# A list scheduler's table and gates changed in a fused attention, expert and MLP kernel, with one layer in plain float32

## The chip, the cores and the metric

The kernel runs on one core of one Trainium2 chip. A core has a tensor engine (PE, its weight loads are shown as PEld), a vector engine (DVE), a scalar engine (ACT), GpSimd (POOL), a queue that issues transfers (SP), and 16 DMA engines that all queues share. The metric is the device time of one execution in microseconds (us). The time before is the median of three runs, 1221.68 us.

## What is computed

Three stages follow each other: attention, a router with capacity that gives each of 1792 tokens to one of 8 experts, and one MLP on all tokens.

```python
x = attn(q, k, v)                      # 1792 tokens x 768
logits = x @ w_gate                    # 1792 x 8
for idx in argsort(-logits.flatten()): # best pair first
    tok, e = idx // 8, idx % 8
    if assigned[tok] >= 0 or counts[e] >= 224: continue
    assigned[tok] = e; counts[e] += 1
for e in range(8):
    out[e's tokens] = relu(x[e's tokens] @ w1[e]) @ w2[e]   # 768 -> 1024 -> 768
h = out @ w_in                         # 768 -> 2048
return (h * cos(h)) @ w_out            # 2048 -> 768
```

## The kernel before, in words

The kernel records steps, each with an engine, an estimated duration, and what it reads and writes, and a list scheduler (`Plan.run`) then writes them out in an order for each engine. That order is final: on the chip every engine takes its instructions in this order and waits at each for what it needs. There are two plans. The first holds attention and the start of the router; the second, `moe`, everything from the first expert on.

**The second plan.** Eight router *phases* each find the tokens of one expert. Phases 0 and 1 search by counting (`quick`), phases 2 to 7 by bisection (`slow`). `route(t, behind)` records phase t, the load of the expert's number, two gathers of 112 rows of x each into `xr` (POOL) and their transposes into `xe`. `expert(t, j)` has a first layer of 8 blocks of 18 matmuls 128x128 by 224 columns (`acc<-xe,wx`) and a second one of 6 blocks of 24 (`acc<-gh,wx`, 224 columns). Two experts make a group, and `mlp` then takes the group's 448 columns: 16 blocks of 18 (`acc<-x2h,wx` and `x2l`, below M1), 6 blocks of 48 (`acc<-gh,wx` and `gl` with 448 columns, below M2).

**Three products.** Every such matmul is done as three in fp32r: each operand is split in a rounded part and a rest. An expert's weights come as float32 into `ws` (ring of 4), ACT writes the rounded part and DVE the rest into `wx` (ring of 4): `weights`, lines 1176 to 1194. The MLP's weights were split before and are loaded as they are.

**A bisection phase** writes its 56 KB table `vm` to DRAM (`rows`), and eight copies on SP read it back, each spread over 16 partitions (`AB<-rows`, lines 987 to 992). Then eight search steps follow: DVE compares (`oh<-AB`, two halves), ACT counts, DVE makes `ind`, PE sums over partitions (`rt<-ind,bd`), DVE sets the next bound. At the end come `M`, a prefix sum, `rel`, `pv` and 16 small matmuls (`rt<-pv,oh`) that give `idx`, the row numbers for the gathers.

The step costs of these transfers are numbers in the code: an SP issue 0.5 us, a copy 0.4 us of bus, and 1.1 us from the bus to landing for all transfers.

```python
            if s.dma is not None:
                bus = max(bus, st + (1.1 if w[0] == "SP" else 2.0)) + s.dma
                s.end = bus + 1.1
```

Phases 2, 4 and 6 may begin only after a step named by `behind`: the last matmul block of the group's second expert (`chain[-1]`). Two `memset`s on POOL write one element of the third and fourth buffer of `ws` after the first gathers.

Of the kernel before, what the change touches and what calls it, by code (L numbers as in the profile page):

```python
# [23 lines left out]


class Step:
    __slots__ = ("ways", "after", "before", "late", "wait", "ready", "end", "eng", "dma", "start", "rush", "mode", "pad")

    def __init__(self, ways, dma):
        self.ways, self.dma, self.rush = ways, dma, 0.0  # L30
        self.after, self.before = {}, []
        self.wait, self.ready, self.end, self.late = 0, 0.0, 0.0, None

# [17 lines left out]
class Plan:  # L51
# [51 lines left out]
        hi = lo + 1 + sum(s * (n - 1) for s, n in free)  # L103
        return x.name, p, p + n, lo * size, hi * size

    def add(self, ways, reads, writes, dma=None):

        if self.group is not None:
            self.group.append((ways[0], reads, writes))
            return  # L110
        s = Step(ways, dma)
        s.mode, s.pad = None, self.pad * (ways[0][0] == "PE")
        if ways[0][0] == "PE" and isinstance(reads[0], bass.AP):
            w = reads[0]
            s.mode = (w.partition_size() <= D, 32 if w.free_size() <= 32 else 64 if w.free_size() <= 64 else 128)
        s.rush = self.rush + self.ahead * (ways[0][0] != "DVE")
        for x in reads:
            self.touch(s, x, False)
        for x in writes:
            self.touch(s, x, True)  # L120
        self.steps.append(s)
# [47 lines left out]
    def run(self, order, prefer=0.0, edge=1.0, lag=2.6, hold=0.7, by=6.0, queue=9e9, more=0.0,  # L169
            same=0.0):  # L170

        for s in self.steps:
            s.wait = len(s.after)
            for t in s.after:
                t.before.append(s)
        nxt = dict(order)  # L180
        for s in reversed(self.steps):
            e, d = s.ways[0][0], min(w[1] for w in s.ways)
            d += lag if s.dma is not None else 0.0
            late = 0.0
            for t in s.before:
                late = min(late, t.late - SYNC.get((e, t.ways[0][0]), 0.17) - (
                    edge if e != t.ways[0][0] else 0.0))
            if s in nxt:
                late = min(late, nxt[s].late - more * d)
            s.late = late - d  # L190
        for s in self.steps:
            s.late -= s.rush
        free, bus, mode = {}, 0.0, None
        avail = [s for s in self.steps if s.wait == 0]
        idx = {s: i for i, s in enumerate(self.steps)}
        out = []
        while avail:
            best = None
            for e in ("PE", "DVE", "ACT", "POOL", "SP"):
                least = free.get(e, 0.0) if e != "SP" else max(free.get(e, 0.0), bus - 1.1 - queue)  # L200
                mine = [(max(least, s.ready), s, w) for s in avail for w in s.ways if w[0] == e]
                if not mine:
                    continue
                good = []
                for st, s, w in mine:
                    f = st + w[1]
                    if len(s.ways) > 1:
                        f += prefer * w[1] * (e == "DVE")
# [24 lines left out]
            if s.dma is not None:  # L233
                bus = max(bus, st + (1.1 if w[0] == "SP" else 2.0)) + s.dma
                s.end = bus + 1.1
            out.append((st, idx[s], w[2]))
            for t in s.before:
                t.ready = max(t.ready, s.end + SYNC.get((s.eng, t.ways[0][0]), 0.17) + t.pad)
                t.wait -= 1
                if t.wait == 0:  # L240
                    avail.append(t)
        assert len(out) == len(self.steps)
        for _, _, f in sorted(out, key=lambda o: o[:2]):
            f()
# [457 lines left out]
class Router:  # L702
# [276 lines left out]
    def slow(self):  # L979
# [5 lines left out]
        v.tensor_tensor(vm, vt, P["m"].unsqueeze(1).to_broadcast([CP, E, NCOL]), op=ALU.min)  # L985
        rows, sync = self.rows, nc.nc.sync
        nc.add([("SP", 0.5, lambda: sync.dma_start(rows.rearrange("e (p c) -> p e c", c=NCOL), vm))], [vm], ["rows"],
               dma=1.5)
        for e in range(E):
            nc.add([("SP", 0.5, lambda e=e: sync.dma_start(V[16 * e:16 * e + 16],  # L990
                                                           rows[e:e + 1].to_broadcast([16, NCOL * CP])))],
                   ["rows"], [V[16 * e:16 * e + 16]], dma=0.4)
        b, KX, ti, h = P["b"], P["KX"], P["ti"], NCOL * CP // 2
        for s in range(8):
            src = P["b0"]
# [101 lines left out]
C1 = 6.28125  # L1097
C2 = 2.0 * math.pi - C1
TUNE_B = (1.75, 0.8, 2.6, 0.6, 7.0, 9e9)
RUSH = (15.0, 0.0, 5.0)  # L1100
QUICK = (0, 1)
WARM_B = 24
GATE = 2
AHEAD = 100.0
TURN = 5
GROUPS = [[0, 1], [2, 3], [4, 5], [6, 7]]


def moe(tc, P, R, ident, x_rows, w1, w2, w_in, w_out, out, narrow):

    nc = tc.nc
    with ExitStack() as ctx:
# [12 lines left out]
        obuf = ring("o", 1, [128, PT])  # L1125
        rows = ring("xr", 2, [CP, DM])
        xe = cst.tile([128, KD, PT], F32R, name="xe")
        xo = cst.tile([CP, 4, DM], F32, name="xo")
        x2h = cst.tile([128, KD, PT], F32R, name="x2h")
        x2l = cst.tile([128, KD, PT], F32R, name="x2l")  # L1130
# [8 lines left out]
        def route(t, behind):  # L1139
# [9 lines left out]
            xr = []  # L1149
            for h in range(2):  # L1150
                x = rows()
                P.add([("POOL", 1.03, lambda x=x, h=h: nc.gpsimd.indirect_dma_start(  # L1152
                    out=x, out_offset=None, in_=x_rows,
                    in_offset=bass.IndirectOffsetOnAxis(ap=idx[t][:, h:h + 1], axis=0)))], [idx[t]], [x], dma=0.96)
                xr.append(x)
            R.close()
            if t == 0:
# [5 lines left out]
                P.rush = RUSH[0]  # L1163
                for _ in range(GATE):
                    stage()
                for _ in range(4 - GATE):
                    o = stage()[0:1, 0, 0:1]
                    P.add([("POOL", 0.04, lambda o=o: nc.gpsimd.memset(o, 0.0))], xr, [o])
            for q in range(3):
                p = turn() if t or q < 2 else acc()  # L1170
                for j in range(2):
# [3 lines left out]
                        P.tensor.transpose(p[:, o:o + CP], xr[h][:, d * 128:(d + 1) * 128], ident[0:CP, 0:CP])  # L1175
                src = p[:, 0:PT].rearrange("p (j s) -> p j s", j=2)
                hi, lo = xe[:, 2 * q:2 * q + 2, 0:CAP], xe[:, 2 * q:2 * q + 2, CAP:PT]
                sc.activation(hi, src, AF.Copy)
                v.tensor_tensor(lo, src, hi.bitcast(F32), op=ALU.subtract)

        def weights(src, c0, n, keys):

            s, x = stage()[:, 0:n], parts()[:, 0:n]
            hi, lo = x[:, :, 0], x[:, :, 1]

            def load():
                w = src()
                nc.sync.dma_start(s, w[:, c0:c0 + 128].rearrange("(k p) n -> p k n", p=128))

            P.add([("SP", 0.46, load)], keys, [s], dma=n * 0.182)  # L1190
            P.add([("ACT", 0.093 + n * 0.1067, lambda: nc.scalar.activation(hi, s, AF.Copy)),  # L1191
                   ("DVE", 0.07 + n * 0.0667, lambda: nc.vector.tensor_copy(hi, s))], [s], [hi])
            v.tensor_tensor(lo, s, hi.bitcast(F32), op=ALU.subtract)
            return hi, lo
# [19 lines left out]
        def expert(t, j):  # L1214
# [1 line left out]
                return lambda: w[bass.ds(ev[t], 1)].rearrange("o k n -> (o k) n")  # L1216

            for f in range(K1):
                hi, lo = weights(of(w1), f * 128, KD, [f"ev{t}"])
                p = acc()[:, 0:CAP]  # L1220
                for d in range(KD):
                    block(lambda: three(p, hi[:, d], lo[:, d], xe[:, d, 0:CAP], xe[:, d, CAP:PT], d == 0, d == KD - 1))
                a, b = hT[:, f, 0:CAP], hT[:, f, CAP:PT]
                sc.activation(a, p, AF.Relu)
                v.scalar_tensor_tensor(b, p, 0.0, a.bitcast(F32), op0=ALU.max, op1=ALU.subtract)
# [59 lines left out]
            nc.gpsimd.memset(apart, 0.0)  # L1285

        P.shared = False
        narrow.plan(P, cst, len(narrow.todo))
        behind = None

        def fetch(t, step=None):
# [6 lines left out]
        for grp in GROUPS:  # L1298
            for j, t in enumerate(grp):
                if j:  # L1300
                    fetch(t)
                expert(t, j)
            behind = chain[-1]
            mlp(grp, lambda: fetch(grp[-1] + 1, behind))
        P.run(zip(chain, chain[1:]), *TUNE_B)

# [64 lines left out]
```

## Time and profile before

| what | us |
|---|---|
| median of three runs (1220.99 to 1222.58) | 1221.68 |
| the profiled execution, its own time | 1224.71 |
| its span, first to last instruction | 1222.9 |
| PE busy in the span | 1142.1 |
| DVE busy | 852.9 |
| ACT busy | 657.5 |

The profiled execution took 1.8 us more than its span, and 3.0 us more than the median of the runs. Attention fills the first 365 us, the switch to the experts lies from 365 to 450 us, and the rest is a row of experts and MLP groups in which PE is nearly always busy. A busy PE isn't PE at its peak: a matmul's record is longer than the distance to the next one.

### The profile page before, as it was taken

The page shows a single profiled execution, that of the slowest core. Times are in us where ns is not written, and L with a number is a line of the kernel's source. Part 1 is how long each engine was busy: PE and PEld are TensorE (multiplying, and loading weights), DVE is VectorE, ACT ScalarE, POOL GpSimd, SP SyncE. Part 2 cuts the span into 40 slices and gives each one's busy share as a digit, 9 for nine tenths or more (in the row PEclk, how much of TensorE's full clock was granted, in tenths as well). Part 3 has the DMA queues.
Part 4 walks back from the last instruction along what each step waited for, and adds up shares of the span by engine and source line. Part 5 has one row for each costly group of instructions (what it writes and reads, how often), then busy time and mean ns, then how long its engine had stood idle before and what let it go on. Part 6 is the DMA issues. An engine that isn't in the chain of part 4 may idle for free.

```text
span 1222.9 us, 23588 instructions
## 1 busy us (share of the span) xinstructions
PE 1142.1 (93%) x8712; PEld 947.5 (77%) x8712; DVE 852.9 (70%) x2335; ACT 657.5 (54%) x1576; POOL 150.3 (12%) x287
## 2 busy tenths in 40 slices
PE   7999999999985989998999999899999899999996
PEld 4555655565543889887899988799988789999996
DVE  6998999999958865794576498277579458546401
ACT  5976877776643533781455384255468155435400
POOL 5532324241000000000001000002000001100001
PEclk8999999999995889999999999899999999899999
DMA  8357666766642656779468767838776856766761
GB/s 203 115 165 226 209 209 189 247 232 219 215 141 63 166 154 205 236 241 245 163 164 241 209 214 251 257 91 228 218 245 233 240 192 162 207 197 211 233 216 60
DMA packets 181395, 241.86 MB, mean 198 GB/s; under 512 B 14176, under 2 KB 156960, under 8 KB 175136
## 3 DMA queue, kind: packets, MB, share of 16 engines
q1 hardware_dynamic: 178720, 229.35, 61.1%
q0 software_dynamic: 2560, 11.01, 3.2%
q8 instruction: 68, 1.11, 0.4%
q14 instruction: 47, 0.39, 0.1%
HBM read 203.71 MB, written 36.52 MB: 196 GB/s over the span
## 4 chain that ended last, share of the span: by engine, by line
PE 50%; DVE 27%; DMA 13%; ACT 6%; issue 3%; POOL 1%; SPq 1%; POOLq 0%; DVEq 0%; ACTq 0%
PE acc L47 35%; DVE r L47 4%; DVE cm L47 4%; PE po L47 3%; PE st L47 3%; DMA xr<-x,idx 3%; DVE na L47 3%; ACT oh L47 3%; DVE oh L47 3%; DMA AB<-rows 3%; PE s L47 2%; PE dn L47 2%; PE tr L47 2%; DVE wx L47 1%; DMA ws<-in_moe_w_dram 1%
## 5 line engine op out<-in xcount | busy, mean ns | idle before, releaser
L47 PE MATMUL acc<-gh,wx 128*128 128x224 f32 (+1 forms) x1952 | 374.9, 317 | 0.0
L47 PEld LDWEIGHTS acc<-gh,wx 128*128 128x128 f32 x1952 | 286.5, 195 | 24.7 <-issue 13.1
L47 PE MATMUL acc<-x2h,wx 128*128 128x448 f32 x768 | 223.6, 369 | 0.0
L47 DVE TENSOR_TENSOR wx<-ws,wx 128x768 fp32r<-128x768 f32 (+1 forms) x112 | 120.0, 1071 | 64.5 <-ACT wx L1191 64.5
L1191 ACT ACTIVATE wx<-ws 128x768 fp32r<-128x768 f32 (+1 forms) x112 | 104.7, 936 | 109.6 <-PE acc L47 69.6
L47 PEld LDWEIGHTS acc<-x2h,wx 128*128 128x128 f32 x768 | 144.6, 188 | 15.5 <-issue 3.1
L47 ACT ACTIVATE oh<-oh 128x896 bf16<-128x896 bf16 x96 | 90.4, 942 | 107.0 <-DVE oh L47 105.5
L47 PE MATMUL acc<-gl,wx 128*128 128x448 f32 (+1 forms) x400 | 146.1, 365 | 0.0
L47 PE MATMUL acc<-x2l,wx 128*128 128x448 f32 x384 | 140.7, 366 | 0.0
L47 PE MATMUL acc<-xe,wx 128*128 128x224 f32 x1152 | 137.1, 280 | 0.6 <-DVE wx L47 0.5
L47 PEld LDWEIGHTS acc<-xe,wx 128*128 128x128 f32 x1152 | 134.4, 196 | 1.3 <-DVE wx L47 0.7
L47 ACT ACTIVATE pf<-st 112x448 f32<-112x448 f32 x192 | 93.4, 537 | 38.7 <-PE st L47 36.5
L47 DVE TENSOR_REDUCE cm<-s 128x1 f32<-128x448 f32 x168 | 99.5, 616 | 5.2 <-PE s L47 3.8
L1152 POOL DMA_INDIRECT xr<-x,idx x16 | 17.7, 1107 | 652.7 <-issue 215.9
L47 DVE TENSOR_SCALAR oh<-AB,b 128x896 bf16<-128x896 f32 x96 | 61.6, 683 | 50.5 <-DMA AB<-rows 34.4
L47 PE MATMUL st<-qq,kk 64*112 64x448 f32 x576 | 92.3, 391 | 2.3 <-ACT pf L47 2.2
L47 ACT ACTIVATE r<-r 128x448 f32<-128x448 f32 x128 | 72.8, 573 | 36.5 <-DVE r L47 35.1
L47 PE MATMUL po<-pf,vr 112*64 112x448 f32 x384 | 84.5, 560 | 0.0
L47 PEld LDWEIGHTS acc<-gl,wx 128*128 128x128 f32 x400 | 77.4, 193 | 5.2
L47 PEld LDWEIGHTS acc<-x2l,wx 128*128 128x128 f32 x384 | 72.2, 188 | 5.8
L47 PEld LDWEIGHTS st<-qq,kk 64*112 64x112 f32 x576 | 49.4, 171 | 25.7 <-ACT pf L47 10.1
L47 DVE SCALAR_TENSOR_TENSOR na<-nr,na 128x384 int32<-128x384 int32 (+1 forms) x112 | 68.0, 632 | 0.5
(237 smaller groups left out, 1662.5 us busy)
## 6 DMA issues: line engine op xcount, KB each, us to landing
wx<-w_in SPq DMA_DIRECT2D x64, 768.0 KB
wx<-w_out SPq DMA_DIRECT2D x48, 1024.0 KB
ws<-in_moe_w_dram SPq DMA_DIRECT2D x64, 384.0 KB
ws<-in_moe_w_dram SPq DMA_DIRECT2D x48, 512.0 KB
nr<-in_moe_w_in_dram SPq DMA_DIRECT2D x32, 384.0 KB
w_in<-nr SPq DMA_DIRECT2D x32, 384.0 KB
nr<-in_moe_w_out_dram SPq DMA_DIRECT2D x24, 512.0 KB
w_out<-nr SPq DMA_DIRECT2D x24, 512.0 KB
```

Source lines behind the costliest of these rows:

```text
L47: self.plan.add([(self.eng, self.plan.cost(self.eng, name, out, r, kw), lambda: f(*args, **kw))], r, w)
L1152: P.add([("POOL", 1.03, lambda x=x, h=h: nc.gpsimd.indirect_dma_start(out=x, out_offset=None, in_=x_rows, in_offset=bass.IndirectOffsetOnA ...
L1191: P.add([("ACT", 0.093 + n * 0.1067, lambda: nc.scalar.activation(hi, s, AF.Copy)), ("DVE", 0.07 + n * 0.0667, lambda: nc.vector.tensor_co ...
```

## The change

Four things change. The scheduler gets, for three kinds of transfers, other issue costs and a time from issue to landing (`land`). The step that phases 2, 4 and 6 may follow is 90 blocks earlier in the chain, which is 6 blocks after the start of the group's second expert. The first expert's first layer is taken in plain float32: its weights go from `ws` straight to PE, its input is kept in one tile `xf`, and one matmul takes the place of three. The two gates on `ws` copy an element of the gathered rows in place of writing a zero. A call of `narrow.plan` that had no work left is dropped, and phase 1 gets 4 us of urgency.

```diff
@@ Plan.run
-            d += lag if s.dma is not None else 0.0
+            d += (lag if s.land is None else s.land) if s.dma is not None else 0.0
...
-                s.end = bus + 1.1
+                s.end = bus + 1.1 if s.land is None else st + w[1] + s.land
@@ Router.slow
         nc.add([("SP", 0.5, lambda: sync.dma_start(rows..., vm))], [vm], ["rows"],
-               dma=1.5)
+               dma=0.2, land=2.8)
         for e in range(E):
-            nc.add([("SP", 0.5, lambda e=e: sync.dma_start(V[16 * e:16 * e + 16], ...
-                   ["rows"], [V[16 * e:16 * e + 16]], dma=0.4)
+            nc.add([("SP", 0.85, lambda e=e: sync.dma_start(V[16 * e:16 * e + 16], ...
+                   ["rows"], [V[16 * e:16 * e + 16]], dma=0.4, land=8.0)
@@
-RUSH = (15.0, 0.0, 5.0)
+RUSH = (15.0, 4.0, 5.0)
+EARLIER = 90
@@ route
-                P.add([("POOL", 1.03, lambda x=x, h=h: nc.gpsimd.indirect_dma_start(
+                P.add([("POOL", 2.1 - 0.9 * h, lambda x=x, h=h: nc.gpsimd.indirect_dma_start(
...
+                    land=5.0)
-                for _ in range(4 - GATE):
+                for h in range(4 - GATE):
                     o = stage()[0:1, 0, 0:1]
-                    P.add([("POOL", 0.04, lambda o=o: nc.gpsimd.memset(o, 0.0))], xr, [o])
+                    P.add([("POOL", 0.1, lambda o=o, h=h: nc.gpsimd.tensor_copy(o, xr[h][0:1, 0:1]))], xr, [o])
...
+                if t == 0:
+                    copy = v.tensor_copy if q == 1 else lambda o, i: sc.activation(o, i, AF.Copy)
+                    copy(xf[:, 2 * q:2 * q + 2], src)
+                    continue
@@ expert
             for f in range(K1):
+                if t == 0:
+                    s = whole(of(w1), f * 128, KD, [f"ev{t}"])
+                    p = acc()[:, 0:CAP]
+                    for d in range(KD):
+                        block(lambda: P.tensor.matmul(p, s[:, d], xf[:, d], start=d == 0,
+                                                      stop=d == KD - 1))
+                else:
...
@@ end of moe
-        narrow.plan(P, cst, len(narrow.todo))
...
-            behind = chain[-1]
+            behind = chain[-EARLIER]
```

What this does to the order is seen at three places. The attention plan keeps its order on PE.

PE, from the last matmul of phase 1's row numbers (`rt<-pv,oh`, in the first expert) to the transposes of the second expert's gathered rows (`tr<-ident,xr`; xr_4688 holds the first gather, xr_4689 the second), before:

```order
L47 MATMUL rt_4672<-pv,oh 112x6
L47 MATMUL acc_4667<-gh,wx_4681 128x224 x15
L47 MATMUL acc_4668<-gh,wx_4678 128x224 x24
L47 MATMUL acc_4669<-gh,wx_4679 128x224 x9
L47 MATMUL tr_4670<-ident,xr_4688 128x112 x2
L47 MATMUL tr_4671<-ident,xr_4688 128x112 x2
L47 MATMUL acc_4669<-gh,wx_4679 128x224 x3
L47 MATMUL tr_4670<-ident,xr_4689 128x112 x2
L47 MATMUL tr_4671<-ident,xr_4689 128x112 x2
L47 MATMUL acc_4669<-gh,wx_4679 128x224 x12
```

The same place in the changed kernel:

```order
L47 MATMUL rt_4672<-pv,oh 112x6
L47 MATMUL acc_4667<-xf,ws_4677 128x224 x5
L47 MATMUL acc_4668<-gh,wx_4678 128x224 x24
L47 MATMUL acc_4669<-gh,wx_4679 128x224 x24
L47 MATMUL acc_4666<-gh,wx_4680 128x224 x9
L47 MATMUL tr_4670<-ident,xr_4688 128x112 x2
L47 MATMUL acc_4666<-gh,wx_4680 128x224 x9
L47 MATMUL tr_4670<-ident,xr_4689 128x112 x2
L47 MATMUL acc_4666<-gh,wx_4680 128x224 x6
L47 MATMUL acc_4667<-gh,wx_4681 128x224 x6
```

Phase 1's row numbers now stand within the first layer (`xf,ws`); 5 float32 matmuls and 57 others lie between them and the first transposes (48 before), and 9 between the first and the second gather's transposes (3 before); 78 matmuls of the first expert are left behind those.

SP, from the last first-layer weights of the second expert to the MLP's first weights (`ws` are the expert's tiles, those of 8x128 the second layer's; `wx<-w_in` the MLP's), before:

```order
L1188 DMA ws_4676<-in_moe_w_dram 128x8x128
L1188 DMA ws_4677<-in_moe_w_dram 128x8x128
L1188 DMA ws_4674<-in_moe_w_dram 128x8x128
L1188 DMA ws_4675<-in_moe_w_dram 128x8x128
L1188 DMA ws_4676<-in_moe_w_dram 128x8x128
L1188 DMA ws_4677<-in_moe_w_dram 128x8x128
L1199 DMA wx_4678<-w_in_67 128x1536
L1199 DMA wx_4679<-w_in_67 128x1536
L1199 DMA wx_4680<-w_in_67 128x1536
L1199 DMA wx_4681<-w_in_67 128x1536
L987 DMA rows<-vm 112x8x16
L990 DMA AB<-rows 16x1792 x8
```

And in the changed kernel:

```order
L1194 DMA ws_4676<-in_moe_w_dram 128x8x128
L1194 DMA ws_4677<-in_moe_w_dram 128x8x128
L1194 DMA ws_4674<-in_moe_w_dram 128x8x128
L987 DMA rows<-vm 112x8x16
L1194 DMA ws_4675<-in_moe_w_dram 128x8x128
L990 DMA AB<-rows 16x1792 x8
L1194 DMA ws_4676<-in_moe_w_dram 128x8x128
L1194 DMA ws_4677<-in_moe_w_dram 128x8x128
L1211 DMA wx_4678<-w_in_67 128x1536
L1211 DMA wx_4679<-w_in_67 128x1536
```

Phase 2's table and its eight copies now stand ahead of the second expert's last two weight tiles, and not behind four MLP tiles. Phases 4 and 6 move likewise in the later groups.

PE at the start of the MLP, in the changed kernel (`rt<-ind,bd` is the first search step of phase 2):

```order
L47 MATMUL acc_4666<-gh,wx_4680 128x224 x24
L47 MATMUL acc_4667<-gh,wx_4681 128x224 x24
L47 LDWEIGHTS bd
L47 MATMUL rt_4673<-ind,bd 128x1
L47 MATMUL acc_4668<-x2h,wx_4678 128x448
L47 MATMUL acc_4668<-x2l,wx_4678 128x448
```

Before, 84 of M1's matmuls stand ahead of this step; now none. The later steps move with it: phase 2's `rt<-pv,oh` stands behind 18 matmuls of M2 (57 before), phase 3's first step behind 102 (123 before), and phase 3's `rt<-pv,oh` behind 60 first-layer matmuls of the next expert (84 before), while its transposes keep their place in that expert's second layer. The groups behind repeat this.

## Rows read from the trace of the kernel before

**Rows 1.** The page's part 2: the granted clock of PE in 40 slices.

```profile
PEclk8999999999995889999999999899999999899999
```

**Rows 2.** Waits of PE, longest first: us in total, times, longest us.

```profile
PE rt L47 <- DVE ind L47: 15.8, 5, 4.8
PE tr L47 <- DMA xr<-x,idx: 11.0, 8, 2.7
PE rt L47 <- DVE pv L47: 5.6, 4, 4.2
```

**Rows 3.** Timeline of PE: start, us, what, idle before and releaser.

```profile
577.23 0.16 PE L47 MATMUL rt<-ind,bd 128*128 128x1 bf16 x1 [4.81 <-DVE ind L47]
```

**Rows 4.** Pieces of the chain that ended last: start, us, what, count.

```profile
101.49 1.66 PE po L47 x8
...
577.39 7.44 PE acc L47 x24
584.86 4.97 PE acc L47 x24
...
977.30 6.54 PE acc L47 x24
...
1042.32 6.59 PE acc L47 x39
```

**Rows 5.** Busy time of the engines in two stretches, then PEclk, DMA share, GB/s.

```profile
460.00:470.00 10.00, 10.00 (x92) 10.00 (x91) 6.83 (x12) 6.31 (x10) 0.00 (x0) 1.00 0.89 250
...
510.00:520.00 10.00, 10.00 (x51) 8.84 (x50) 9.78 (x22) 9.33 (x20) 0.00 (x0) 1.00 0.63 220
```

**Rows 6.** Timeline of SP, 487 to 575 us.

```profile
489.37 4.24 SPq L990 DMA_DIRECT2D AB<-rows  x8
...
555.95 0.33 SPq L987 DMA_DIRECT2D rows<-vm  x1
...
559.36 6.99 SPq L990 DMA_DIRECT2D AB<-rows  x8
```

**Rows 7.** Timeline of DVE: phase 3's first search step.

```profile
574.11 1.28 DVE L47 TENSOR_SCALAR oh<-AB,b 128x896 bf16<-128x896 f32 x2 [14.70 <-DMA AB<-rows]
576.90 0.28 DVE L47 TENSOR_SCALAR ind<-cnt,rp 128x1 bf16<-128x1 f32 x1 [1.51 <-ACT oh L47]
```

**Rows 8.** Busy time, 393.7 to 437.3 us (phase 1): all instructions, columns as in rows 5.

```profile
393.70:437.30 43.60, 40.11 (x327) 37.70 (x326) 39.26 (x169) 24.74 (x58) 1.99 (x4) 0.87 0.58 161
```

**Rows 9.** Timeline of DVE: weight splits and phase 1's row numbers.

```profile
397.71 0.95 DVE L47 TENSOR_TENSOR wx<-ws,wx 128x768 fp32r<-128x768 f32 x1
...
437.28 0.17 DVE L47 CAST idx<-row 112x2 int32<-112x2 f32 x1
...
474.91 1.23 DVE L47 TENSOR_TENSOR wx<-ws,wx 128x1024 fp32r<-128x1024 f32 x1 [1.15 <-ACT wx L1191]
```

**Rows 10.** Timeline of PE, 441 to 485 us: transposes, second expert's first matmuls, M1's first.

```profile
444.41 0.61 PE L47 MATMUL tr<-ident,xr 112*128 112x112 f32 x4 [1.91 <-DMA xr<-x,idx]
...
447.56 1.01 PE L47 MATMUL tr<-ident,xr 112*128 112x112 f32 x4 [2.20 <-DMA xr<-x,idx]
...
451.56 0.75 PE L47 MATMUL acc<-xe,wx 128*128 128x224 f32 x2
...
484.45 0.38 PE L47 MATMUL acc<-x2h,wx 128*128 128x448 f32 x1
```

**Rows 11.** A group of PEld by shape: busy us, mean ns of one.

```profile
L47 PEld LDWEIGHTS acc<-xe,wx 128*128 128x128 f32 x1152 | 134.4, 196 | 1.3 <-DVE wx L47 0.7 <-DVE xe L47 0.3 <-DVE gh L47 0.2
```

**Rows 12.** Timeline of PE: transposes of later experts that waited for gathers.

```profile
639.83 0.51 PE L47 MATMUL tr<-ident,xr 112*128 112x112 f32 x3 [0.75 <-DMA xr<-x,idx]
...
1041.49 0.82 PE L47 MATMUL tr<-ident,xr 112*128 112x112 f32 x3 [2.74 <-DMA xr<-x,idx]
```

**Rows 13.** Chain pieces: an expert's 384 KB weight tile, issue to landing.

```profile
389.56 3.86 DMA ws<-in_moe_w_dram
...
558.91 7.12 DMA ws<-in_moe_w_dram
```

More of the change, by code (lines that the diff above doesn't have):

```diff
@@ L26, with __init__ @@
 class Step:
-    __slots__ = ("ways", "after", "before", "late", "wait", "ready", "end", "eng", "dma", "start", "rush", "mode", "pad")
-    def __init__(self, ways, dma):
-        self.ways, self.dma, self.rush = ways, dma, 0.0
+    __slots__ = ("ways", "after", "before", "late", "wait", "ready", "end", "eng", "dma", "start", "rush", "mode", "pad", "land")
+    def __init__(self, ways, dma, land):
+        self.ways, self.dma, self.land, self.rush = ways, dma, land, 0.0
         self.after, self.before = {}, []
@@ L104, in key, with add @@
         return x.name, p, p + n, lo * size, hi * size
-    def add(self, ways, reads, writes, dma=None):
+    def add(self, ways, reads, writes, dma=None, land=None):
         if self.group is not None:
@@ L110, in add @@
             return
-        s = Step(ways, dma)
+        s = Step(ways, dma, land)
         s.mode, s.pad = None, self.pad * (ways[0][0] == "PE")
@@ L987, in slow @@
         nc.add([("SP", 0.5, lambda: sync.dma_start(rows.rearrange("e (p c) -> p e c", c=NCOL), vm))], [vm], ["rows"],
-               dma=1.5)
+               dma=0.2, land=2.8)
         for e in range(E):
-            nc.add([("SP", 0.5, lambda e=e: sync.dma_start(V[16 * e:16 * e + 16],
+            nc.add([("SP", 0.85, lambda e=e: sync.dma_start(V[16 * e:16 * e + 16],
                                                            rows[e:e + 1].to_broadcast([16, NCOL * CP])))],
-                   ["rows"], [V[16 * e:16 * e + 16]], dma=0.4)
+                   ["rows"], [V[16 * e:16 * e + 16]], dma=0.4, land=8.0)
         b, KX, ti, h = P["b"], P["KX"], P["ti"], NCOL * CP // 2
@@ L1127, in moe @@
         xe = cst.tile([128, KD, PT], F32R, name="xe")
+        xf = cst.tile([128, KD, CAP], F32, name="xf")
         xo = cst.tile([CP, 4, DM], F32, name="xo")
@@ L1151, in route @@
                 x = rows()
-                P.add([("POOL", 1.03, lambda x=x, h=h: nc.gpsimd.indirect_dma_start(
+                P.add([("POOL", 2.1 - 0.9 * h, lambda x=x, h=h: nc.gpsimd.indirect_dma_start(
                     out=x, out_offset=None, in_=x_rows,
-                    in_offset=bass.IndirectOffsetOnAxis(ap=idx[t][:, h:h + 1], axis=0)))], [idx[t]], [x], dma=0.96)
+                    in_offset=bass.IndirectOffsetOnAxis(ap=idx[t][:, h:h + 1], axis=0)))], [idx[t]], [x], dma=0.96,
+                    land=5.0)
                 xr.append(x)
@@ L1177, in route, with whole @@
                 hi, lo = xe[:, 2 * q:2 * q + 2, 0:CAP], xe[:, 2 * q:2 * q + 2, CAP:PT]
+                if t == 0:
+                    copy = v.tensor_copy if q == 1 else lambda o, i: sc.activation(o, i, AF.Copy)
+                    copy(xf[:, 2 * q:2 * q + 2], src)
+                    continue
                 sc.activation(hi, src, AF.Copy)
                 v.tensor_tensor(lo, src, hi.bitcast(F32), op=ALU.subtract)
-        def weights(src, c0, n, keys):
-            s, x = stage()[:, 0:n], parts()[:, 0:n]
-            hi, lo = x[:, :, 0], x[:, :, 1]
+        def whole(src, c0, n, keys):
+            s = stage()[:, 0:n]
             def load():
@@ L1190, in weights @@
             P.add([("SP", 0.46, load)], keys, [s], dma=n * 0.182)
+            return s
+        def weights(src, c0, n, keys):
+            s, x = whole(src, c0, n, keys), parts()[:, 0:n]
+            hi, lo = x[:, :, 0], x[:, :, 1]
             P.add([("ACT", 0.093 + n * 0.1067, lambda: nc.scalar.activation(hi, s, AF.Copy)),
@@ L1218, in expert @@
             for f in range(K1):
[L1219 to L1222, printed above, removed]
+                if t == 0:
[5 more added lines that the diff above has]
+                else:
+                    hi, lo = weights(of(w1), f * 128, KD, [f"ev{t}"])
+                    p = acc()[:, 0:CAP]
+                    for d in range(KD):
+                        block(lambda: three(p, hi[:, d], lo[:, d], xe[:, d, 0:CAP], xe[:, d, CAP:PT], d == 0,
+                                            d == KD - 1))
                 a, b = hT[:, f, 0:CAP], hT[:, f, CAP:PT]
```

## The prediction

> **What bounds the kernel now.** I looked first at the granted clock over the span [rows 1]: it is low where attention hands over to the experts (slices 12 to 14, 367 to 459 us), and an 8 stands in two later slices, 764 to 795 and 1040 to 1070 us. So most of the span runs at the full clock and PE is the limit there; what can be won lies in the hand-over and in a few stops. The list of PE's waits names them [rows 2]: 15.8 us in five waits for `ind`, the first count of a bisection search; 11.0 us for gathered rows; 5.6 us for `pv`, of which one of 4.2 us is phase 0's and stays.
>
> A wait costs more than its length. The longest one ends at 577.23 us [rows 3]. The 24 matmuls behind it take 7.44 us, the next 24 take 4.97 [rows 4]: the first dozen runs at half the clock (1.2 in place of 2.4 GHz). That is 2.5 us, a second case in the next group is like it, a third is 6.54 against 4.97, 1.6 us [rows 4]. After the last gather wait 39 matmuls take 6.59 us [rows 4], 2.3 us more than 39 cost at the full clock, where a matmul takes 10/92 = 0.109 us with 224 columns and 10/51 = 0.196 us with 448 [rows 5]. I move along PE's order with these two.
>
> **First search steps: 15.8 us of waits and 6.6 us of clock.** Before, phase 3's table leaves at 555.95 us, its eight copies are issued from 559.36 to 566.35 [rows 6], DVE can compare at 574.11 and `ind` is there at 577.2 [rows 7]: 21.2 us after the table. PE has 66 M2 matmuls (123 - 57), 13 us, between phase 2's row numbers and this step, which is why it stands 4.8 us. In the changed order there are 84 (102 - 18), 16.5 us, and the table goes out earlier: in DVE's order `vm` comes ahead of the epilogue of M1's last block, so some 2 us before M2 starts. PE reaches the step 102 x 0.196 + about 1 us for the row numbers' 16 small matmuls = 21 us after M2's start, 23 us after the table. 21.2 are needed, so the wait goes. Phase 2's first step: `vm` stands in DVE's order behind the third of the second expert's first-layer epilogues, about 8 us into an expert of 288 matmuls, 31.3 us. With the same 21.2 us its count is ready 29 us in, 2 us ahead of M1. Groups 2 and 3 repeat both. I remove all 15.8 us, and with them the 2.5 + 2.5 + 1.6 = 6.6 us of clock. Bounds: if the copies land 4 us later than in the case shown, about 2 us come back at each of five places, 10 us; none can come out better than zero.
>
> **`pv`: 1.4 us.** Three short waits (5.6 - 4.2) go, because phase 2's row numbers now are behind 18 M2 matmuls, 3.5 us, with `pv` some 2.6 us into M2. Bound: they stay.
>
> **Later gathers: 6.2 us.** The transposes of the odd phases keep their place and the row numbers move 24 first-layer matmuls ahead: 24 x 0.109 = 2.6 us. That covers the 0.75 us wait [rows 12], one like it in the next group (0.6), and 2.6 of the last group's 3.2 (2.74 and a short one before). With the 2.3 us of clock: 0.75 + 0.6 + 2.6 + 2.3 = 6.2. Bounds: 1 to 6.8.
>
> **The first expert: 6.4 us.** From 393.7 to 437.3 us phase 1 keeps DVE busy for 39.26 of 43.6 us [rows 8], so DVE sets when `idx` comes, at 437.28 [rows 9]. The change takes away the eight first-layer splits there, 8 x 0.95, and moves four second-layer ones of about 1.15 us behind `idx` (DVE's order keeps one of five ahead of it): 7.6 + 4.6 = 12.2 us, so for DVE `idx` could come at 425.1. PE then decides. A float32 matmul leaves two records; a chain piece shows eight `po` records (four matmuls of 448 columns, two and two beside each other on half the array) in 1.66 us [rows 4], so 0.83 for a pair, 0.41 us for 224 columns. 48 of these are 19.8 us in place of 144 x 0.109 = 15.7. Before the row numbers PE must do 43 of them (17.6), the counting matmuls (I estimate 4) and lose some 2 us to the half clock, from 402 on as before: 425.6, and about 1 us for the row numbers themselves. I take `idx` at 426.5, 10.8 us earlier.
>
> Gathered rows arrive for the first transposes 7.1 us after `idx` (444.41 - 437.28) and for the second 10.3 us after [rows 9, 10], so at 433.6 and 436.8. PE comes to the first after 5 x 0.41 + 57 x 0.109 = 8.3 us, no wait, and to the second 1.3 us later, a wait of about 1.5 us in place of 1.91 and 2.20. Then 78 x 0.109 + 1.5 us of transposes: the second expert starts at 446.8, before at 451.56 [rows 10], 4.8 us earlier. It took 32.9 us to M1 (484.45 - 451.56), and 31.3 without the low clock behind those waits: 1.6 more, together 6.4. The ACT work that goes is worth nothing by itself: ACT is busy 24.7 of 43.6 us [rows 8]. The gates on `ws` now wait until rows land; the third tile is needed 5 us after that and takes 3.86 [rows 13], so nothing. Bounds: 0.37 us for a float32 matmul (8 us saved in all) and the rival below.
>
> **What is added: 3 us.** The table and its copies stand ahead of the second expert's two last weight tiles on SP. The table leaves 8.3 us into the expert, the copies start 2.1 to 3.4 us later and take 4.24 to 6.99 us to issue [rows 6], so the next tile is issued at 15 to 19 us. It lands 3.9 to 7.1 us after that [rows 13] (a third more for its 512 KB: 5 to 9), the split takes ACT and DVE about 1.15 us each [rows 9]: ready at 22.5 to 30.5 us. PE needs it at 31.3 - 2 x 2.6 = 26. So 0 to 4.5 us at each of three experts; before, the last split ended at 476.1, 5.7 us ahead of its use (a block of 24 before 484.45). I take 1 us each.
>
> **Sum.** 15.8 + 6.6 + 1.4 + 6.2 + 6.4 - 3 = 33.4 us off the profiled execution's 1224.7, 1191.3; the runs' median lies 3.0 lower, so 1188.3. I say 1188.5.
>
> **Rivals.** *Exposed weight loads.* A fp32r load of 128 columns is 0.196 us long [rows 11] and hides behind a matmul, since 92 of both fit in 10 us. If the 96 float32 loads don't hide, they cost up to 96 x 0.196 = 18.8 us, all on the path because PE and DVE end together here: 1207. Against it: the `po` piece has no such room, though its loads are of 64 columns. The Trainium skill, TensorE: Matmul & The Clock Gate, section Weight-path perf modes, says that the fast weight load is not used where the weights are FP32, and its section on LDWEIGHTS gives columns / 1.2, 107 ns for 128; by that alone the loads would add an estimated 96 x 0.107 = 10.3 us and the time would be 1199. No trace here has a 128-column float32 load ahead of a full matmul.
>
> *Late weights.* All three experts stand 4.5 us, and each then pays 2.5 us of clock: 21 us in place of 3, 1206.5. For it: the rows' upper ends all have to meet, as they did around 560 us, where the MLP's 1 MB tiles shared the engines; beside an expert the tiles are half as large. The Trainium skill, DMA: Bandwidth & Descriptors, section Queues, rings and completion order, says that SP's transfers share one ring on each engine and are taken in ring order, so a tile issued behind the copies also waits for their data; the rows' 7.1 us has such a queue in it.
>
> *The search stays late.* If the copies need 5 us longer beside weight traffic, the first steps keep their waits and the clock loss: 22.4 us come back, 1211.
>
> *Slower than before.* SP is one queue in order, so the same two tiles wait for `vm`. If DVE comes to `vm` late, because the splits ahead of it wait for PE, every second expert stands. It must cost 33.4 + 3 = 36 us over three experts, 12 us each: with 2.5 us of clock, 9.5 us of standing, a tile ready at 35.5 us and not at 26. From there the change loses; with 2 us more each it ends at 1228. No row has a tile that late.
>
> **How the numbers follow.** Chances: the forecast 0.64 (own range 1181 to 1198, by the bounds of the float32 price, the tiles and the gathers), exposed loads 0.11, late weights 0.14, search stays late 0.07, slower 0.04. The range 1181 to 1208 holds the first three but for part of their ends, about 0.8. 0.2%, 2.4 us, is about what a measurement of this kernel can tell from no change. Faster 0.94, within 0.02, slower 0.04.
>
> **What would show it.** Right: no wait of PE for `ind` over 2 us; 24 matmuls behind the first step of phase 3 in 5 us; the second expert's first matmul near 447; float32 records at 0.2 us each; no wait of PE for `wx` over 1.5 us near the end of the second, fourth and sixth expert. Wrong: a first layer of 30 us and more in the first expert, SP standing before the copies beside an expert, or long waits for `wx`.

## The result and the profile of the changed kernel

The changed kernel takes 1191.51 us (median of four runs, 1186.61 to 1195.54) and the kernel before 1222.13 beside it: ratio 0.9747, 95% interval 0.9705 to 0.979. The forecast was 1188.5. The medians lie 30.6 us apart. The profiled executions lie further apart, 38.1 us: that of the changed kernel is the lowest of the four (1186.61 us, span 1184.8), and that of the kernel before, 1224.71, is slower than all four beside it. The page's part 2 shows the granted clock in 40 slices:

```profile
PEclk8999999999997799999999999999999999999998
```

Against [rows 1] the low stretch is two slices (355 to 415 us) and not three, and the two slices further on with an 8 are gone; the last slice, a 9 before, is an 8. The list of PE's waits (us in total, times, longest):

```profile
PE rt L47 <- DVE pv L47: 5.4, 2, 4.2
PE tr L47 <- DMA xr<-x,idx: 3.3, 2, 2.4
PE tr L47 <- DVE xo L47: 1.6, 2, 1.1
PE rt L47 <- DVE ind L47: 0.2, 1, 0.2
```

Of [rows 2], 15.8 us for `ind` are 0.2, and 11.0 us for gathered rows are 3.3, both before the second expert. The chain has the matmuls behind phase 3's first search step, which took 7.44 us in [rows 4]:

```profile
560.92 4.97 PE acc L47 x24
```

To place the gain I cut the span at three kinds of marks on PE's timeline: the first matmul of phase 0's row numbers, the first matmul of each M1, and the end. In the kernel before (its first M1 is in [rows 10]):

```profile
389.27 2.61 PE L47 MATMUL rt<-pv,oh 112*112 112x6 bf16 x16 [4.25 <-DVE pv L47]
...
685.63 0.37 PE L47 MATMUL acc<-x2h,wx 128*128 128x448 f32 x1
...
886.80 0.37 PE L47 MATMUL acc<-x2h,wx 128*128 128x448 f32 x1
...
1089.84 0.37 PE L47 MATMUL acc<-x2h,wx 128*128 128x448 f32 x1
```

In the changed kernel:

```profile
387.91 2.61 PE L47 MATMUL rt<-pv,oh 112*112 112x6 bf16 x16 [4.25 <-DVE pv L47]
...
479.38 0.45 PE L47 MATMUL acc<-x2h,wx 128*128 128x448 f32 x1
...
670.51 0.45 PE L47 MATMUL acc<-x2h,wx 128*128 128x448 f32 x1
...
861.55 0.45 PE L47 MATMUL acc<-x2h,wx 128*128 128x448 f32 x1
...
1053.64 0.38 PE L47 MATMUL acc<-x2h,wx 128*128 128x448 f32 x1
```

| us | before | changed | gain |
|---|---|---|---|
| attention, to the first mark | 389.3 | 387.9 | 1.4 |
| hand-over, to the first M1 | 95.2 | 91.5 | 3.7 |
| three groups, M1 to M1 | 605.4 | 574.3 | 31.1 |
| last M1 to the end of the span | 133.1 | 131.2 | 1.9 |

The sum is 38.1. The first and the last line are no work of the change (below). The groups gave more than forecast and the hand-over less.

### The profile page after: what moved, and what is told of

It is laid out like the page before. It is cut to its first block, busy times and chain, and to the rows that moved or that the text cites. A ratio compares the mean times of both kernels' runs of the same rounds, so it can differ in the third digit from the quotient of the medians.

```text
span 1184.8 us, 23438 instructions
## 1 busy us (share of the span) xinstructions
PE 1126.2 (95%) x8664; PEld 936.1 (79%) x8664; DVE 845.5 (71%) x2328; ACT 651.7 (55%) x1564; POOL 150.6 (13%) x287
## 4 chain that ended last, share of the span: by engine, by line
PE 70%; DVE 17%; DMA 8%; ACT 3%; issue 2%; POOL 0%; SPq 0%; POOLq 0%; DVEq 0%; ACTq 0%
PE acc L47 54%; PE po L47 4%; PE st L47 4%; DVE cm L47 3%; DVE na L47 3%; PE s L47 2%; PE dn L47 2%; DMA ws<-in_moe_w_dram 2%; DMA qk<-in_q_dram 2%; PE t L47 1%; PE tr L47 1%; DVE oh L47 1%; PE rt L47 1%; DVE nr L47 1%; DVE AB L47 1%
## 5 line engine op out<-in xcount | busy, mean ns | idle before, releaser
L47 PE MATMUL acc<-gh,wx 128*128 128x224 f32 (+1 forms) x1952 | 366.4, 313 | 0.0
L47 PEld LDWEIGHTS acc<-gh,wx 128*128 128x128 f32 x1952 | 280.7, 191 | 10.5
L47 DVE TENSOR_TENSOR wx<-ws,wx 128x768 fp32r<-128x768 f32 (+1 forms) x104 | 112.3, 1080 | 69.9 <-ACT wx L1203 69.3
L1203 ACT ACTIVATE wx<-ws 128x768 fp32r<-128x768 f32 (+1 forms) x101 | 95.5, 946 | 98.7 <-PE acc L47 55.3
L47 PE MATMUL acc<-gl,wx 128*128 128x448 f32 (+1 forms) x400 | 143.0, 357 | 0.0
L47 ACT ACTIVATE pf<-st 112x448 f32<-112x448 f32 x192 | 93.6, 538 | 41.1 <-PE st L47 38.9
L47 PE MATMUL acc<-xe,wx 128*128 128x224 f32 x1008 | 114.4, 275 | 0.0
L47 PEld LDWEIGHTS acc<-xe,wx 128*128 128x128 f32 x1008 | 113.6, 192 | 0.1
```

Of the source, the lines that this page charges most:

```text
L47: self.plan.add([(self.eng, self.plan.cost(self.eng, name, out, r, kw), lambda: f(*args, **kw))], r, w)
```

## The experiments

The profiled executions, cut at the same marks, with the median of each kernel and its ratio to the kernel before, measured beside it. "Costs" are the scheduler's new transfer numbers, "early" the 90 blocks, "urgent" phase 1's 4 us. Every kernel but the one before has the new gates on `ws` and goes without the dropped call; no run tests these alone.

| kernel | costs | early | float32 | urgent | median us | ratio (95%) | hand-over | groups | last |
|---|---|---|---|---|---|---|---|---|---|
| before | | | | | 1222.1 | | 95.2 | 201.2 201.2 203.0 | 133.1 |
| changed | x | x | x | x | 1191.5 | 0.9747 (0.9705, 0.979) | 91.5 | 191.1 191.0 192.1 | 131.2 |
| again | x | x | x | x | 1187.6 | 0.9741 (0.9722, 0.9759) | 90.3 | 190.8 190.8 190.8 | 131.2 |
| again_2 | x | x | x | x | 1189.3 | 0.9752 (0.9724, 0.9779) | 91.7 | 191.2 191.6 190.8 | 133.3 |
| no_early | x | | x | x | 1201.5 | 0.9844 (0.9823, 0.9866) | 88.7 | 195.4 194.7 194.7 | 133.1 |
| old_costs | | x | x | x | 1227.7 | 1.0071 (1.0042, 1.0099) | 92.1 | 204.3 204.8 203.4 | 133.2 |
| no_f32 | x | x | | x | 1194.9 | 0.9795 (0.977, 0.9819) | 98.4 | 191.8 190.8 190.8 | 133.2 |
| only_f32 | | | x | | 1215.6 | 0.9949 (0.9925, 0.9972) | 90.6 | 200.1 198.3 202.5 | 133.4 |
| only_costs | x | | | | 1199.3 | 0.9824 (0.9789, 0.9858) | 89.4 | 196.6 194.7 197.6 | 131.2 |
| only_early | | x | | | 1229.4 | 1.0063 (1.0045, 1.0082) | 93.6 | 199.4 206.4 205.5 | 131.2 |
| no_f32_no_rush | x | x | | | 1186.5 | 0.9734 (0.9699, 0.9769) | 88.5 | 190.9 190.7 190.8 | 133.2 |
| no_rush | x | x | x | | 1187.6 | 0.9735 (0.9705, 0.9764) | 90.2 | 191.0 192.0 190.7 | 131.3 |
| land_t1 | x | x | x | x | 1193.6 | 0.9765 (0.9731, 0.98) | 93.3 | 193.7 191.1 190.8 | 133.1 |
| early_60 | x | 60 | x | x | 1198.5 | 0.9815 (0.9789, 0.984) | 91.4 | 193.7 191.8 196.8 | 133.2 |

Each expectation names a theory A and a rival B that this run can tell apart; they are not the same from run to run.

**again.** The changed kernel once more.

> The changed kernel, unaltered, for its spread. Its four runs lie 9 us apart (1186.6 to 1195.5), those of before 2.5. Theory A (waits for rows and weights that come back in some runs, each with a stretch at half the clock): values again between 1186 and 1196, and the profile, if it is one of the slower ones, shows stops of PE for xr or wx at the first, second or last expert that the first profile has not. Rival B (attention differs from run to run): the stages behind 450 us take the same time and the difference lies ahead of 365 us.

1187.61 us, groups of 190.8 us three times. The gain isn't jitter of attention: attention ended 3.9 us later than in the first profile, and the ratio is the same. What spread the first four runs over 9 us isn't shown, since these five lie within 3.9.

**no_early.** Only the starting point is put back.

```diff
-            behind = chain[-EARLIER]
+            behind = chain[-1]
```

> Undoes the earlier begin of phases 2, 4, 6 alone (chain[-1] again); new costs and the float32 layer stay. PE's order then has the first search step behind 123 M1 matmuls and the odd phases' row numbers only 78 matmuls, 8.5 us, ahead of their transposes. Theory A (both parts of the order are needed): no wait for ind over 1 us, but gather waits of 2 to 4 us at experts 3, 5 and 7 with some 2.5 us of clock each: 1199 to 1207. Rival B (the costs alone take the waits away): 1190 to 1194.

1201.51, as A said. The waits for `ind` stay gone; what comes back is a stop for gathered rows in each group, since the search ends later. PE's timeline:

```profile
635.47 0.41 PE L47 MATMUL tr<-ident,xr 112*128 112x112 f32 x2 [1.96 <-DMA xr<-x,idx]
...
831.73 0.41 PE L47 MATMUL tr<-ident,xr 112*128 112x112 f32 x2 [3.00 <-DMA xr<-x,idx]
...
1026.44 0.41 PE L47 MATMUL tr<-ident,xr 112*128 112x112 f32 x2 [2.43 <-DMA xr<-x,idx]
```

**old_costs.** The costs are put back, the rest stays.

```diff
-               dma=0.2, land=2.8)
+               dma=1.5)
...
-            nc.add([("SP", 0.85, lambda e=e: ...            dma=0.4, land=8.0)
+            nc.add([("SP", 0.5, lambda e=e: ...             dma=0.4)
...
-                P.add([("POOL", 2.1 - 0.9 * h, lambda ...   dma=0.96, land=5.0)
+                P.add([("POOL", 1.03, lambda ...            dma=0.96)
```

> Undoes the new transfer costs alone; phases still begin early and the float32 layer stays. PE's order has phase 2's first search step 36 matmuls ahead of the end of the second expert, where its count is some 2 us late by the forecast's reckoning, and phase 1's row numbers 42 matmuls ahead of the transposes. Theory A (costs and begin both count): waits for ind of about 2 us at three places and 2 us more for the first gathers: 1196 to 1203. Rival B (the early begin alone is the gain): 1190 to 1194.

1227.68: both missed, the kernel is slower than before. With an earlier start and copies that are believed to land soon after their issue, the steps again stand too close behind them: phase 2's first one 36 matmuls ahead of M1, phase 3's 114 into M2. The search of phase 3 then ends late as well, and its rows are waited for. PE's timeline of the first group:

```profile
476.12 0.16 PE L47 MATMUL rt<-ind,bd 128*128 128x1 bf16 x1 [1.78 <-DVE ind L47]
...
568.47 0.16 PE L47 MATMUL rt<-ind,bd 128*128 128x1 bf16 x1 [4.22 <-DVE ind L47]
...
636.41 0.82 PE L47 MATMUL tr<-ident,xr 112*128 112x112 f32 x3 [4.16 <-DMA xr<-x,idx]
```

So the early start without the costs is worth nothing (only_early, below, shows it alone); it is the costs that make use of it.

**no_f32.** The first expert's first layer is split again; costs, early start and urgency stay.

```diff
-                if t == 0:
+                if False:
                     s = whole(of(w1), f * 128, KD, [f"ev{t}"])
```

> Undoes the float32 first layer alone: the first expert splits its first-layer weights again and takes three products. Theory A: phase 1's row numbers come some 11 us later and the second expert starts 4 to 6 us later; later stages as in the changed kernel: 1195 to 1199. Rival B (the layer's gain is eaten by the gathers, which then run beside more weight loads): 1190 to 1194.

1194.92, at A's near end, all of it in the hand-over (98.4 us; the changed kernel has 90.3 to 91.7). It looked as if the float32 layer were worth 7 us. That reading fell with the runs below.

**only_f32, only_costs, only_early.** One part alone each (no urgency in any of them).

> The float32 layer with the gates that copy an element; step costs, the place from which phases 2, 4 and 6 may begin and the urgency of phase 1 are those of the kernel before, and so are PE's places of all search steps from the first MLP on. Theory A (parts add up): with the costs the float32 layer was worth 1194.9 - 1187.6 = 7.3 us, so 1219.5 - 7.3: 1210 to 1214. The waits for the first count and the half clock after them stay (about 16 us in five). Rival B (the layer pays only where the costs move the row numbers and gathers to where they are ready): 1217 to 1220, with the gain lost in waits for gathered rows of the second expert.

> New step costs alone: the first layer stays split, phases 2, 4 and 6 may not begin early. PE reaches phase 2's first step 123 first-layer matmuls into the MLP (84 before) and phase 3's 129 matmuls into the second layer or a little less. Theory A (parts add up): costs with float32 gave 18.0 us, float32 is 7.3 of it, so 10.7 us: 1207 to 1211, with waits for the first count under 2 us in all. Rival B (the costs give their gain only together with an earlier start, since the search then ends too late for the next expert's row numbers): 1214 to 1220, with long waits for the row numbers' operand or for gathered rows.

> The earlier start alone, with the step costs of the kernel before: PE meets phase 2's first search step inside the second layer of the second expert. Theory A (with the old costs the scheduler believes the copies land in about 2 us, so it puts the first step far too early, PE stands there and behind it, and each group pays for it): slower than before as the kernel with float32 and the early start was, 1226 to 1238, with over 15 us of waits for the first count. Rival B (that loss came from the float32 layer together with the old costs, around the hand-over): 1215 to 1221.

1215.63, 1199.33 and 1229.4. only_early agrees with A. only_f32 lies between the two expectations, with a hand-over 4.6 us shorter and 13.7 us of waits for `ind` (15.8 before). only_costs misses both, for the better: A had said 1207 to 1211, as 18.0 less 7.3. It is as fast as no_early, which has the float32 layer and the urgency on top, and its hand-over of 89.4 us is shorter than that of the changed kernel. So with the new costs the two together add nothing there, and the loss of no_f32 needed another cause. The urgency was the one part left.

**no_f32_no_rush, no_rush.** The urgency is taken out, without and with the float32 layer.

```diff
-RUSH = (15.0, 4.0, 5.0)
+RUSH = (15.0, 0.0, 5.0)
```

> New step costs and the earlier start, with the split first layer and without phase 1's 4 us of urgency. In the run without the float32 layer but with that urgency the way from phase 0's row numbers to the first MLP matmul was 98.4 us, with both 90.3 and 91.5, and with the new costs alone (no float32, no urgency) 89.4. Theory A (the float32 layer is worth some 7 us, since it takes DVE's eight splits away): 96 to 99 us on that way, 1193 to 1198 in all. Rival B (the urgency alone made the split layer late; the float32 layer is worth nothing): 88.5 to 91 us on that way, 1186 to 1191 in all.

> The changed kernel without phase 1's urgency. Phase 1's row numbers stand 12 second-layer matmuls later on PE than in the changed kernel. Theory A (float32 sets the hand-over, the urgency does nothing): 1186 to 1191, the way from phase 0's row numbers to the first MLP matmul 90 to 92 us. Rival B (with float32 the urgency pays, as without it it cost): 2 to 4 us slower than the changed kernel, 93 to 95 us on that way.

1186.46 and 1187.61, beside again_2 with 1189.32: B in the first, A in the second. Without urgency the split layer's hand-over is 88.5 us, with it 98.4; the intervals of the two ratios (0.9699 to 0.9769 and 0.977 to 0.9819) just don't touch. Windows of no_f32 over its hand-over (columns as in [rows 5]):

```profile
410.00:420.00 10.00, 8.07 (x64) 7.75 (x62) 9.00 (x43) 4.55 (x14) 0.00 (x0) 0.81 0.48 135
420.00:430.00 10.00, 9.41 (x71) 9.18 (x70) 7.78 (x27) 5.22 (x8) 0.00 (x0) 0.85 0.53 143
430.00:440.00 10.00, 8.59 (x71) 8.46 (x71) 8.86 (x29) 2.61 (x4) 4.33 (x2) 0.83 0.59 171
440.00:450.00 10.00, 8.02 (x59) 7.71 (x59) 6.04 (x17) 3.20 (x6) 0.00 (x0) 0.85 0.92 223
```

and the same of no_f32_no_rush:

```profile
410.00:420.00 10.00, 8.89 (x94) 8.62 (x92) 9.13 (x47) 6.58 (x18) 0.00 (x0) 1.00 0.48 136
420.00:430.00 10.00, 10.00 (x92) 9.95 (x91) 9.86 (x33) 5.38 (x8) 0.00 (x0) 1.00 0.96 260
430.00:440.00 10.00, 8.87 (x87) 8.70 (x87) 9.50 (x37) 2.02 (x4) 2.10 (x2) 1.00 0.40 103
440.00:450.00 10.00, 9.23 (x83) 8.87 (x81) 6.95 (x15) 5.48 (x10) 0.00 (x0) 1.00 0.96 242
```

The urgency moves search work on DVE and PE ahead of first-layer work: PE meets phase 1's third count 18 first-layer matmuls sooner and waits 1.57 us for it. From 400 to 410 us both kernels have a clock of 0.83. With the urgency PE stands for 0.6 to 2.0 us in each of the four windows shown, the granted clock stays at 0.81 to 0.85, and 59 to 71 matmuls get into a window; without it PE stands for 0 to 1.1 us, the clock is 1.00, and 83 to 94 do. The row numbers that it was to hurry come no sooner: `idx` is there 44.7 us after phase 0's row numbers with the urgency and 42.5 without. In the float32 kernels the urgency shows no loss (no_rush).

**land_t1.** The second expert's gathers count 8.5 us.

```diff
-                    land=5.0)
+                    land=8.5 if t == 1 else 5.0)
```

> The changed kernel with one number more: the second expert's gathers count 8.5 us from issue to landing, all others 5.0. Their transposes then stand 84 and 90 matmuls behind phase 1's row numbers (57 and 66 in the changed kernel), all else in its place. Theory A (the late rows cost their wait, 2.4 + 0.9 us, and about 1 us of half clock behind it): 3 to 4.5 us faster than the changed kernel, 1183 to 1185, no wait for gathered rows over 0.5 us before the second expert. Rival B (the wait covers work that is late anyway: the weights of the second expert's first layer or its split come no earlier, so the stop moves behind the transposes): 1186.5 to 1189.

1193.56 (1185.93 to 1197.05), no gain: above both expectations, with a stop behind the transposes as B had it, but for another reason. PE's timeline:

```profile
429.23 10.52 PE L47 MATMUL acc<-gh,wx 128*128 128x224 f32 x84
...
444.27 0.74 PE L47 MATMUL tr<-ident,xr 112*128 112x112 f32 x4 [1.72 <-DVE xe L47]
```

The transposes find their rows, but the third one now waits 1.72 us for DVE, which copies the ones before it (`xe`). The 84 matmuls ahead take 10.52 us where 84 at the full clock (0.112 us each, below) take 9.4, and a late weight tile makes the first group 2.9 us longer.

**early_60.** Starts 30 blocks later.

```diff
-EARLIER = 90
+EARLIER = 60
```

> The changed kernel with 60 in place of 90: phases 2, 4 and 6 may begin 30 blocks later, and their first search step stands 39 first-layer matmuls into the MLP. Theory A (90 blocks is more than needed; the copies then stand behind the second expert's last tiles and no weight tile is late): 1185.5 to 1188, no late tile near the end of the second expert of a group, groups of 190.8 us each. Rival B (the search then ends too late for the next expert's rows, as with no earlier start at all): groups of 192 to 195 us, 1190 to 1200.

1198.45: B. Stops for gathered rows are back in the groups (4.3 us in three waits, the longest 2.9), and the copies now stand right ahead of the MLP's first tiles: M1 waits 0.63 and 0.26 us for `wx<-w_in` at its start in two groups.

**again_2.**

> The changed kernel once more, beside the three others. Theory A: 1186.5 to 1191.5, as in its two series so far (medians 1191.5 and 1187.6); groups of 190.8 us where no weight tile is late, 1 to 3 us more in a group where one is. Rival B (the spread comes from the hand-over, not from the groups): three groups of 190.8 and a way from phase 0's row numbers to the first MLP matmul that differs from 90.3 and 91.5 by over 2 us.

1189.32, in A's range. A weight tile came late in the hand-over (waits of 0.17 and 0.78 us) and in the second group (0.56 us): 191.6 us, not 1 to 3 us more but 0.8. The first group has 191.2 with no wait over 0.1 us.

## Why the prediction was right, and where its steps were not

**First search steps.** Right. No wait for `ind` is over 0.2 us, and 24 matmuls behind phase 3's first step take 4.97 us. The 2 us to spare at phase 2's first step weren't there, though: the count came 24 us after the table and not 21.2, since SP began the copies 5.3 us after the table and not 2.1 to 3.4, and PE met it with nothing to spare. SP's timeline from the table on, and PE's first step:

```profile
455.33 0.84 SPq L987 DMA_DIRECT2D rows<-vm  x1
456.84 0.67 SPq L1194 DMA_DIRECT2D ws<-in_moe_w_dram  x1
460.60 4.13 SPq L990 DMA_DIRECT2D AB<-rows  x8
464.99 1.04 SPq L1194 DMA_DIRECT2D ws<-in_moe_w_dram  x2
```

```profile
479.35 0.16 PE L47 MATMUL rt<-ind,bd 128*128 128x1 bf16 x1 [0.18 <-DVE ind L47]
```

**Clock.** Mis-sized. A group without a late tile is 190.8 us (again), three of them 572.4, so 33.0 us left the groups of before; their waits were 21.6 us (15.8 for `ind`, 4.5 for rows, 1.3 for `pv`). The rest, 11.4, is what the clock took; the forecast had 6.6 + 2.3 = 8.9. The waits between the first and the last M1 of the kernel before ([rows 2] has those for `ind`):

```profile
PE tr L47 <- DMA xr<-x,idx: 4.5, 4, 2.7
PE rt L47 <- DVE pv L47: 1.3, 3, 0.5
```

Its windows with a granted clock under 1.00 between these marks give about the same: 10 us x (1 - clock) over these seven is 11.9, and some of that may fall on time in which PE stood anyway.

```profile
570.00:580.00 10.00, 5.19 (x20) 4.47 (x20) 3.63 (x10) 2.80 (x5) 0.00 (x0) 0.79 1.06 304
580.00:590.00 10.00, 10.00 (x46) 8.80 (x45) 2.42 (x8) 3.12 (x8) 0.00 (x0) 0.87 0.64 243
770.00:780.00 10.00, 5.28 (x24) 4.62 (x24) 2.63 (x9) 1.98 (x4) 0.00 (x0) 0.86 1.07 278
780.00:790.00 10.00, 10.00 (x43) 8.91 (x42) 3.32 (x9) 3.95 (x8) 0.00 (x0) 0.80 0.76 288
970.00:980.00 10.00, 6.62 (x31) 5.83 (x30) 3.62 (x10) 2.89 (x6) 0.00 (x0) 0.93 1.08 304
980.00:990.00 10.00, 10.00 (x48) 8.85 (x47) 3.32 (x11) 3.04 (x8) 0.00 (x0) 0.90 0.79 279
1040.00:1050.00 10.00, 8.51 (x54) 8.51 (x55) 4.43 (x8) 3.53 (x6) 0.00 (x0) 0.66 0.58 148
```

**`pv` and later gathers.** Right: behind the first M1 the changed kernel has no wait for either. no_early and early_60 show what holds this up: the whole search must end early, and then the gathers of the odd and the even phases come in time.

**Late weights.** The mechanism is there, the size is smaller. The forecast took 3 us at three places, the ends of the second, fourth and sixth expert; the first of these lies in the hand-over. In the first two profiles of the changed kernel PE waits for no weights there, in again_2 0.95 us in the second expert and 0.56 in the sixth. In land_t1 one group is 2.9 us longer, so 3 us for a single tile can happen too. The tile in the second expert of again_2, on its chain, and PE's waits for its split:

```profile
464.14 7.86 DMA ws<-in_moe_w_dram
```

```profile
473.20 0.48 PE L47 MATMUL acc<-gh,wx 128*128 128x224 f32 x2 [0.17 <-ACT wx L1203]
474.46 5.39 PE L47 MATMUL acc<-gh,wx 128*128 128x224 f32 x46 [0.78 <-DVE wx L47]
```

The tile is issued right behind the eight copies and takes 7.86 us to land. The Trainium skill (DMA: Bandwidth & Descriptors, section Queues, rings and completion order) says that the transfers of one issuing engine share one ring on each DMA engine and that descriptors are taken in ring order; this trace agrees as far as this tile of 512 KB takes 7.86 us and one of 384 KB in the first expert, with no copies ahead, 3.86 [rows 13]. The 7.12 us of [rows 13], which the forecast read as a queue of this kind, are no case of it: that tile is issued at 558.91, ahead of the copies, which begin at 559.36 [rows 6]. The longest group of the changed kernel's first profile (192.1 us) is no case of it either. Its chain runs over a tile issued at 998.91 that takes 8.79 us to land, but this is some 70 us behind the last copies and right behind two gathers. What delayed it wasn't found.

**The first expert.** Here a step failed: the one from `idx` to the second expert and on to M1. What stands ahead of it held. The eight splits went, and `idx` came at 422.63 (437.28 in [rows 9]), 13.3 us earlier as counted from phase 0's row numbers; 10.8 were forecast. The price of a float32 matmul was right, 22 records in 4.41 us, 0.2 us each, so the rival of exposed loads is out. The Trainium skill (TensorE: Matmul & The Clock Gate, section Weight-path perf modes) says that FP32 weights have no fast load; this trace shows no cost of that. DVE's row numbers and PE's timeline:

```profile
422.63 0.17 DVE L47 CAST idx<-row 112x2 int32<-112x2 f32 x1
```

```profile
406.37 4.41 PE L47 MATMUL acc<-xf,ws 128*128 128x224 f32 x22
...
433.15 0.41 PE L47 MATMUL tr<-ident,xr 112*128 112x112 f32 x2 [2.39 <-DMA xr<-x,idx]
...
435.47 0.57 PE L47 MATMUL tr<-ident,xr 112*128 112x112 f32 x2 [0.90 <-DMA xr<-x,idx]
```

But the forecast let the rows come 7.1 and 10.3 us after `idx`, as before. They came 10.5 and 12.8 us after it, beside weight tiles on busy DMA engines (share 0.88 and 1.02 from 420 to 440 us); in again 8.8 and 12.0. The second expert started at 446.85, which looks like the forecast's 446.8 only because attention ended 1.4 us sooner: counted from phase 0's row numbers it is 3.3 us earlier, 4.8 were forecast. From there to M1 took 32.5 us (32.9 before), and the forecast had 31.3. That price was too low: in again the same stretch without a wait takes 32.2, so a matmul of 224 columns costs 0.112 us and not 0.109. The hand-over gained 3.5 to 4.9 us in the three profiles of the changed kernel, 6.4 were forecast, or 5.4 with the 1 us for the second expert's tile.

Nor does an earlier `idx` by itself make the second expert start earlier. In no_f32_no_rush it comes at 433.29, 42.5 us after phase 0's row numbers and 7.8 later than in the changed kernel, and the second expert starts 55.4 us after them, 3.6 sooner. DVE's row numbers and PE's first matmuls of the second expert there:

```profile
433.29 0.17 DVE L47 CAST idx<-row 112x2 int32<-112x2 f32 x1
```

```profile
446.12 4.15 PE L47 MATMUL acc<-xe,wx 128*128 128x224 f32 x35
```

So the float32 layer isn't what gained the hand-over: new costs alone shorten it by 5.8 us, costs and early start by 6.7. The gathers' new cost puts the transposes 72 matmuls behind the row numbers in these two kernels (48 before), and PE hardly waits for rows there any more: 0.5 us in no_f32_no_rush, 6.5 in the kernel before. The layer itself is 4.1 us more of PE by the forecast's prices (19.8 for 15.7). With the new costs it earns some 7 us only beside the urgency, by undoing what the urgency costs. With the old costs, alone, it earns 4.6 us in the hand-over, though PE still waits 4.5 us for rows there; the granted clock from 400 to 420 us is 1.00 in only_f32 and 0.74 and 0.83 in the kernel before. So the parts don't add: each takes away some of the same waits and of the same low clock. How much of each wasn't measured.

**What the change can't have done.** 1.4 us of the first profile's gain are attention, 1.9 us the last stretch. Attention's end lies between 385.9 and 393.7 us in the profiles of all kernels here, and the change keeps its order on PE. So the forecast of 33.4 met 34.8 in the places that it spoke of. That it came so near is in part luck: with each late tile put where it belongs, it had 1.7 us too much in the hand-over and 3.1 too little in the groups, and these offset each other. Between the medians the gain was 30.6, and 33.2 were forecast.

No version here beats the changed kernel by more than the intervals; no_f32_no_rush, with neither float32 nor urgency, equals it. So the costs with the early start make the gain, and the other two parts aren't needed for it.

## What to carry to other kernels

A list scheduler's cost for a transfer is the distance at which it puts the consumer: measure issue to landing in the trace and go by that before it gets any more freedom. Freedom with wrong costs lost 0.6 to 0.7% here, the right costs alone won 1.8% and with the freedom 2.7%. A longer cost isn't always better: 8.5 us for one pair of gathers, which took 9.5 us to land in the first profile, won nothing. When several edits attack one stretch, test each alone and each left out: an edit whose removal costs 7 us may only repair a neighbour. Price a wait of the tensor engine with the half clock behind it; here 21.6 us of waits cost 33.

## What was unexpected

The last group's matmuls of 448 columns run with no wait at a full granted clock and still at two speeds. The chain's last long piece in the changed kernel, in one profile and in again_2:

```profile
1016.61 141.79 PE acc L47 x849
```

```profile
1016.30 143.83 PE acc L47 x849
```

It is the same kernel and the same 849 matmuls, 2.0 us apart; the kernel before has 143.83 too. The difference is spread evenly: from the last M1 on, each 72 matmuls take 14.6 us in the first profile and 14.9 in again_2. Five of the fourteen profiles have the last stretch in 131.2 to 131.3 us, the others in 133.1 to 133.4. What decides it wasn't found.
